# An operation list of a third annealing in a gated linear attention and mixer kernel

## The chip, the cores and the metric

The kernel runs on one core of a Trainium2 chip. The metric is the device time of one execution in microseconds; the number of a kernel is the median of its runs. Five engines work from instruction queues of their own, each strictly in order: TensorE (PE in the profile, its weight loads PEld), VectorE (DVE), ScalarE (ACT), GpSimd (POOL) and SyncE (SP), which here only issues DMAs. They meet through semaphores.

## The reference

Two parts in sequence. The first is a gated linear attention for 4 batches of 8 heads, 768 steps, 48 dimensions:

```python
f = 1.0 / (1.0 + np.exp(-f_logit))
for t in range(S):
    state = f[:, :, t, :, None] * state + np.einsum('bhd,bhe->bhde', k[:, :, t], v[:, :, t])
    y[:, :, t] = np.einsum('bhd,bhde->bhe', q[:, :, t], state)
```

The second is a mixer on the result x, laid out as 4 x 768 x 384: one two-layer product over the steps (768 to 256 and back), added to x, and one over the channels (384 to 1536 and back), added again:

```python
h = np.maximum(xt @ w_tok1, 0.0) @ w_tok2
u = x + h.transpose(0, 2, 1)
return u + np.maximum(u @ w_ch1, 0.0) @ w_ch2
```

## The kernel before

The 768 steps of a batch are cut into six chunks of 128, and two chunks make a pair P (0, 1, 2). For each batch b and pair the attention is a sequence of short operations. ScalarE forms the logarithm of the gates (lines 454 to 459). VectorE or GpSimd adds the two chunks of a pair (`two`, line 467), TensorE sums along the steps by a triangular matrix (lines 479 to 486), VectorE makes `first` (line 499), and ScalarE takes exponentials into `GG` (lines 502 and 519). VectorE multiplies q and k by them (`qk`, line 523; in the trace line 448, the helper's). The products are turned so that dimensions lie on partitions: for batches 0 and 1 by TensorE (line 546), with a copy out of PSUM into `kT` and `qT` (line 550), for batches 2 and 3 by a DMA transpose that SyncE issues (line 531). TensorE forms scores (line 581), which a mask reduces to `AmT` (lines 619 to 624: either VectorE alone, or a ScalarE copy and a GpSimd product), and the sums of k times v of each chunk (line 599). The running state goes from chunk to chunk through VectorE (line 633 for batch 0, 636 to 641 else), and is copied in two pieces into `state_bd` (line 644). The output of a pair is the product with the values (line 665) plus the terms of the state (line 657); it is copied to `x_bf` and `x_nat` (line 692).

The mixer of a batch follows: `tok1` (line 709), its ReLU into `h1T` (line 716), `tok2` (line 725), the sum u in `u_bf` (lines 736 to 751), the turn of u into `uT` in two halves of three chunks (by TensorE, line 766, for batches 0 and 1; by SyncE's DMA transpose, line 755, for batches 2 and 3), `ch1` (line 784, 24 groups of three matmuls) with its ReLU into `zT` (line 789), `ch2` (line 803, three groups of four matmuls for each chunk), the last addition on VectorE (line 814) and the store (line 818). Helper functions issue many of these, so the trace gives copies as lines 434 to 438, ReLUs as 443 and 445, two-input operations as 448 and the addition of the token mixing as 741.

All of this is written down as 1026 operations in a plan: each with the engines that may run it, what it needs, what it makes and which PSUM bank it uses. `ORDER` then says in which order they are taken and where. An entry divided by four is the number of the operation, and the remainder picks one of its possible engines:

```python
for code in ORDER:
    op = self.ops[code // 4]
    e = op.engine = op.engines[code % 4]
```

`Plan.best` goes through the list, gives every operation a start by its own costs, takes a free PSUM bank for it, and puts filler matmuls on a constant (`steady`, line 852) into early gaps of TensorE. What the chip sees of it is one queue for each engine, in the order of the list. The list is written out in the kernel; it came from an annealing that moved entries about against the same costs. Loads of GpSimd and SyncE are operations like the others, and keep among themselves the order in which the plan lists them.

Of the kernel before, what the change touches and what calls it, by code (L numbers as in the profile page):

```python
# [20 lines left out]
TURNED = 2  # L21
NQ = 2
ORDER = (
# [55 lines left out]
)  # L79
KEPT = 3  # L80
SOFT = (0, 1)
# [804 lines left out]
```

## Time and profile before

| | us |
|---|---|
| median of 3 runs | 166.11 (165.8 to 166.11) |
| profiled execution, its own time | 167.62 |
| its span, first to last instruction | 165.9 |
| TensorE busy | 158.6 |
| VectorE busy | 128.8 |
| ScalarE busy | 106.9 |
| GpSimd busy | 61.7 |

The granted TensorE clock was 0.997 of full speed over the span. Read it by stages: batch 0's attention and the loads fill the first 35 us; from then on channel products of one batch are interleaved with the attention of the next. An engine's busy time is a sum over stages with different limits, so the stages, not the sums, say what an engine's time is worth. In the lists of instructions a time is the start, the next number the length, and what stands in brackets is the idle time before it and what ended it.

### The profile page before, as it was taken

What the parts mean: (1) busy time and instruction counts of PE and PEld (TensorE: products, weight loads), DVE (VectorE), ACT (ScalarE), POOL (GpSimd) and SP (SyncE); (2) the same over time, 40 slices, a digit from 0 to 9 for tenths busy, and PEclk for the clock granted to TensorE, in tenths of its full rate; (3) what the DMA queues carried; (4) which work ended last, traced back from release to release, by engine and by line L of the source; (5) the groups of instructions that cost most, each with busy time, mean ns of one, the idle gap of its engine ahead of it and who ended that gap; (6) DMA issues with size and microseconds to landing.
All of it is one profiled execution on the core that took longest, in us unless ns stands there. A gap on an engine that the chain in (4) does not pass through costs nothing.

```text
span 165.9 us, 4990 instructions
## 1 busy us (share of the span) xinstructions
PE 158.6 (96%) x2052; PEld 101.4 (61%) x2052; DVE 128.8 (78%) x284; ACT 106.9 (64%) x231; POOL 61.7 (37%) x86
## 2 busy tenths in 40 slices
PE   7889997999999999999999999999999999999992
PEld 3356765566667766666666765665666665656661
DVE  6748997589999999998999999988599526704331
ACT  3869784797899999999948966384811511623300
POOL 7961799964776820001914514200322020000000
PEclk9999999999999999999999999999999999999998
DMA  4999999999999999457699990991900030690506
GB/s 123 219 177 171 201 210 232 168 206 227 219 225 222 225 242 142 81 98 115 133 224 128 119 155 0 106 213 50 209 19 4 0 59 16 175 325 17 177 31 206
DMA packets 68183, 24.34 MB, mean 147 GB/s; under 512 B 60896, under 2 KB 67296, under 8 KB 68160
## 3 DMA queue, kind: packets, MB, share of 16 engines
q0 software_dynamic: 41856, 13.77, 68.2%
q1 hardware_dynamic: 25776, 10.06, 28.9%
q8 instruction: 16, 0.26, 0.7%
q10 hardware_dynamic: 528, 0.20, 0.4%
q14 instruction: 7, 0.06, 0.1%
HBM read 25.17 MB, written 4.72 MB: 180 GB/s over the span
## 4 chain that ended last, share of the span: by engine, by line
PE 82%; DMA 5%; ACT 4%; DVE 4%; issue 1%; POOL 1%; DVEq 0%; ACTq 0%; POOLq 0%
PE ps L803 28%; PE ps L784 28%; DMA qk_sb<-in_q_dram 5%; PE ps L709 5%; PE ps L725 4%; PE ps L665 3%; PE ps L581 3%; PE ps L657 2%; PE ps L546 2%; PE ps L599 2%; PE ps L766 1%; PE ps L481 1%; ACT state_bd L434 1%; ACT x_nat L434 1%; DVE qk L448 1%
## 5 line engine op out<-in xcount | busy, mean ns | idle before, releaser
L803 PE MATMUL ps<-w_ch,zT 128*128 128x384 bf16 (+2 forms) x300 | 54.0, 320 | 0.0
L784 PE MATMUL ps<-uT,w_ch 128*128 128x384 bf16 x288 | 51.6, 326 | 0.0
L784 PEld LDWEIGHTS <-w_ch 128*128 128x128 bf16 x288 | 27.8, 98 | 17.6
L803 PEld LDWEIGHTS <-zT 128*128 128x128 bf16 x300 | 27.9, 98 | 17.1
L443 ACT ACTIVATE zT<-ps 128x384 bf16<-128x384 f32 x57 | 25.1, 493 | 16.3 <-PE ps L784 16.1
L624 DVE TENSOR_TENSOR AmT<-ps,mask 128x512 bf16<-128x512 f32 x44 | 28.6, 685 | 1.5 <-PE ps L581 1.2
L445 DVE TENSOR_SCALAR zT<-ps 128x384 bf16<-128x384 f32 x39 | 20.6, 553 | 10.0 <-PE ps L784 8.9
L814 DVE TENSOR_TENSOR x_nat<-x_nat,ps 128x384 f32<-128x384 f32 (+2 forms) x25 | 13.1, 534 | 10.5 <-PE ps L803 10.5
L438 POOL CAST state_bd<-state 48x192 bf16<-48x192 f32 x15 | 5.7, 377 | 28.6 <-DVE state L641 25.8
L448 DVE TENSOR_TENSOR qk<-qk_sb,GG 128x768 bf16<-128x768 bf16 x24 | 12.9, 563 | 1.3 <-DMA qk_sb<-in_q_dram 1.3
L502 ACT ACTIVATE GG<-ps 128x384 bf16<-128x384 f32 x24 | 11.2, 485 | 3.5 <-DVE first L499 2.8
L357 POOL DMA_DIRECT2D v_sb<-in_v_dram x12 | 10.7, 894 | 6.3 <-DMA w_ch<-in_moe_w_ch_dram 3.7
L434 ACT ACTIVATE x_bf<-ps 128x384 bf16<-128x384 f32 x15 | 6.9, 483 | 8.5 <-PE ps L657 8.2
L519 ACT ACTIVATE GG<-first 128x384 bf16<-128x384 f32 x24 | 11.7, 517 | 0.2
L741 DVE TENSOR_TENSOR x_nat<-x_nat,ps 128x384 f32<-128x384 f32 x21 | 10.6, 549 | 1.4 <-PE ps L725 1.2
L357 POOL DMA_DIRECT2D qk_sb<-in_k_dram x12 | 10.9, 905 | 1.6 <-POOLq L870 0.8
L434 ACT ACTIVATE u_bf<-x_nat 128x384 bf16<-128x384 f32 x12 | 5.8, 518 | 8.6 <-DVE x_nat L741 8.6
L357 POOL DMA_DIRECT2D qk_sb<-in_q_dram x12 | 10.8, 898 | 0.5 <-DMA qk_sb<-in_q_dram 0.3
L852 PE MATMUL ps<-steady 128*128 128x512 f32 (+1 forms) x20 | 9.8, 610 | 1.0 <-DVE steady L372 1.0
L438 POOL COPY qT<-qJ 128x1024 bf16<-128x1024 bf16 x3 | 3.4, 1149 | 18.8 <-ACT zT L443 18.7
L709 PE MATMUL ps<-x_bf,w_tok 128*128 128x384 bf16 x48 | 10.4, 327 | 0.0
L434 ACT ACTIVATE x_nat<-ps 128x384 f32<-128x384 f32 x20 | 9.3, 492 | 0.1
(87 smaller groups left out, 231.3 us busy)
## 6 DMA issues: line engine op xcount, KB each, us to landing
out_dram<-x_nat SPq DMA_DIRECT2D x23, 192.0 KB, 2.3
f_sb<-in_f_logit_dram POOLq DMA_DIRECT2D x9, 384.0 KB, 8.9
qk_sb<-in_k_dram POOLq DMA_DIRECT2D x12, 192.0 KB, 8.8
qk_sb<-in_q_dram POOLq DMA_DIRECT2D x12, 192.0 KB, 9.0
v_sb<-in_v_dram POOLq DMA_DIRECT2D x12, 192.0 KB, 8.9
w_ch<-in_moe_w_ch_dram POOLq DMA_DIRECT2D x2, 576.0 KB, 9.0
w_ch<-in_moe_w_ch_dram POOLq DMA_DIRECT2D x1, 1152.0 KB, 10.6
f_sb<-in_f_logit_dram SPq DMA_DIRECT2D x2, 384.0 KB, 5.8
```

Source lines behind the costliest of these rows:

```text
L357: lambda eng=eng, into=held(dst[i], P), of=runs(src, b, P): eng.dma_start(out=into, in_=of),
L434: nc.scalar.activation(out_, in_, AF.Copy, bias=0.0, scale=1.0)
L443: nc.scalar.activation(out_, in_, AF.Relu, bias=0.0, scale=1.0)
L445: nc.vector.tensor_scalar(out_, in_, 0.0, None, ALU.max)
L448: (nc.vector if op.engine == DVE else nc.gpsimd).tensor_tensor(out_, a, b_, what)
L502: add(ACT, r, lambda n=n: nc.scalar.activation(GG[i][:, 1, n], sview(), AF.Exp, bias=0.0, scale=2.0 * n - 1.0), need=["tables"] if b == 0 ...
L519: add(ACT, r, lambda n=n: nc.scalar.activation(GG[i][:, 0, n], first[i], AF.Exp, bias=0.0, scale=2.0 * n - 1.0), need=[("first", i)] + ([" ...
L624: add(DVE, r, lambda into=into, made=made, m4=m4: nc.vector.tensor_tensor(into, made(), m4, ALU.mult), need=masks, make=[("AmT", i, js, pa ...
L709: add(PE, rank("tok1", rt), lambda rt=rt, kt=kt, pm=pm: nc.tensor.matmul(banks[pm.at][:, 0:DM], lhsT=w_tok1[:, kt, rt * 128:(rt + 1) * 128 ...
L784: nc.tensor.matmul(banks[pm.at][:, 0:384], lhsT=w[:, kt, c0:c0 + 128], rhs=uT[:, th, :, kt, :], start=(kt == 0), stop=(kt == 2))
L803: nc.tensor.matmul(banks[pm.at][:, 0:n1 - n0], lhsT=zT[:, kt, tt * 128:(tt + 1) * 128], rhs=w_ch2[:, kt, n0:n1], start=(kt == 0), stop=(kt ...
L814: add(DVE, rank("ch2", tt), lambda un=un, pm=pm, n=n1 - n0: nc.vector.tensor_tensor(un, un, banks[pm.at][:, 0:n], ALU.add), make=[("x_nat" ...
```

## The change

Only the list is other: the same 1026 operations in the order of a third annealing with other random numbers and the same objective, in which SyncE's first two loads were then exchanged. On TensorE the same operations stand in another order. 44 operations move from VectorE to ScalarE and 38 from ScalarE to VectorE; 8 move from ScalarE to GpSimd and 7 back, and 2 from VectorE to GpSimd (the sums `two` of pairs 1 and 2 of batch 0). SyncE's list begins in both with the first half of batch 0's gates of pair 0, then those of pair 1 and of pair 2. Its later entries differ: in the new list the store of batch 0's chunk 3 stands earlier, that of its chunk 5 later, and the transposes of batch 3's pair 0 stand behind three stores.

In the opening VectorE's list, from the first product of q and k on, was

```
qk(P0), qk(P0), mask, state c0, kT(P0), mask, state_bd c0, qk(P1), qk(P1), two(P2), ...
```

and is now

```
qk(P0), mask, mask, qk(P0), first(P1), mask, mask, kT(P0), state c0, qT(P0), qk(P1), qk(P1), ...
```

The list itself, cut to its first and last lines:

```diff
 ORDER = (
-    0, 4, 12, 16, 24, 28, 32, 8, 20, 188, 192, 196, 36, 40, 44, 76, 68, 48, 52, 60, 208, 356, 212, 220, 64, 224,
-    236, 240, 228, 360, 364, 368, 248, 244, 216, 376, 232, 372, 380, 388, 260, 80, 84, 265, 384, 200, 88, 296,
-    252, 92, 96, 56, 300, 256, 72, 309, 304, 396, 392, 204, 312, 268, 272, 504, 408, 400, 276, 288, 404, 316,
-    292, 280, 413, 508, 512, 320, 324, 100, 104, 108, 416, 420, 516, 448, 428, 452, 536, 532, 524, 520, 461,
-    457, 544, 540, 112, 116, 120, 284, 124, 128, 132, 432, 136, 328, 332, 340, 440, 344, 464, 336, 468, 348,
...
-    4060, 4000, 4020, 4040, 4072, 4076, 4080, 4084, 4088, 4092, 4096, 4100,
+    0, 4, 12, 16, 8, 20, 24, 28, 32, 188, 192, 196, 80, 88, 92, 96, 357, 100, 104, 36, 40, 44, 48, 76, 52, 208,
+    212, 220, 216, 240, 236, 228, 224, 232, 248, 56, 64, 244, 360, 364, 368, 252, 60, 72, 256, 296, 260, 300,
+    264, 376, 388, 384, 84, 372, 304, 200, 308, 396, 392, 68, 312, 268, 272, 316, 276, 292, 288, 325, 321, 204,
+    380, 400, 408, 280, 413, 405, 108, 112, 116, 120, 124, 128, 132, 505, 284, 508, 512, 328, 332, 516, 341,
+    524, 520, 532, 536, 448, 416, 420, 336, 452, 428, 456, 528, 440, 460, 424, 540, 544, 436, 349, 136, 140,
...
+    3980, 2180, 4056, 4076, 4040, 4060, 4080, 3992, 4084, 4088, 4092, 3996, 4096, 4000, 4100,
 )
```

98 rows, old and new, of the table ORDER are left out of this document.

## The prediction

> **What bounds the kernel now.** I read the stretches first: where the matrix engine is idle decides which part of a reordering can pay at all.
>
> ```profile
> PE 158.6 (96%) x2052; PEld 101.4 (61%) x2052; DVE 128.8 (78%) x284; ACT 106.9 (64%) x231; POOL 61.7 (37%) x86
> 0.00:35.00 35.00, 30.89 (x439) 19.50 (x440) 25.74 (x71) 24.53 (x48) 27.10 (x37) 1.00 1.43 188
> 35.00:145.00 110.00, 110.00 (x1496) 70.87 (x1495) 97.20 (x202) 78.35 (x175) 34.59 (x50) 1.00 0.94 132
> 145.00:165.90 20.90, 17.67 (x121) 11.02 (x119) 5.89 (x12) 4.00 (x10) 0.00 (x0) 0.97 0.44 153
> L852 PE MATMUL ps<-steady 128*128 128x512 f32 (+1 forms) x20 | 9.8, 610 | 1.0 <-DVE steady L372 1.0
> ```
>
> The first row is the page's busy time, the next three are stretches (length; then PE, PEld, DVE, ACT, POOL busy), the last is the filler matmuls that compute nothing. From 35 to 145 us TensorE is busy 110.00 of 110.00 us at clock 1.00: nothing there can be won by order, only lost. Lost time lies ahead of 35 us (35.00 - 30.89 = 4.1 idle, 9.8 of filler) and behind the last matmul. So the second view is the chain of waits through the opening.
>
> ```profile
> 2.34 8.39 DMA qk_sb<-in_q_dram
> 10.85 1.04 DVE qk L448 x2
> 13.28 0.69 DVE kT L436
> 26.53 0.99 issue
> 28.14 0.51 PE ps L665 x32
> 28.93 0.92 PE ps L709 x5
> 29.86 0.50 ACT h1T L443
> 33.62 0.49 PE ps L766 x6
> 34.12 2.93 PE ps L784 x18
> ```
>
> Columns: start, length, what. The opening is a latency chain: batch 0's q lands at 10.73, then products, turns, the chunk-to-chunk state, the value matmuls of pair 2 (28.14), token mixing, the turns of u, and the first channel matmul at 34.12. From there TensorE is fed to the end. The end of the kernel is therefore the time of the first channel matmul, plus the TensorE work then left, plus new stalls.
>
> **The opening, step by step.** Both lists give every engine the same operations up to the landing at 10.73 in what matters: GpSimd's first five loads and SyncE's first three loads stand in the same order in both (so the exchange named in the title is one against the annealing's own result, and costs nothing here). One operation ahead of it moves: pair 1's f32 sum, 0.56 us on VectorE, goes to GpSimd behind its fifth load and delays the loads behind it. They queue for the wire anyway; I take 0.
>
> After the landing, these rows of before are the yardstick:
>
> ```profile
> 4.55 0.20 DVE L412 COPY mask<-tri 64x64 bf16<-64x64 bf16 x1
> 8.97 0.56 DVE L499 TENSOR_TENSOR first<-ps,f_sb 128x384 f32<-128x384 f32 x1 [0.96 <-PE ps L486]
> 12.37 1.02 ACT L434 ACTIVATE qT<-ps 128x1024 bf16<-128x1024 bf16 x1 [1.39 <-PE ps L546]
> 13.70 0.83 ACT L457 ACTIVATE f_sb<-f_sb 128x768 f32<-128x768 f32 x1
> 14.71 0.32 ACT L434 ACTIVATE state_bd<-ps 48x192 bf16<-48x192 f32 x1 [0.17 <-DVE state_bd L436]
> 15.08 0.34 PE L599 MATMUL ps<-v_sb,qk 64*64 64x48 bf16 x11
> 18.43 0.64 PE L581 MATMUL ps<-qT,kT 48*64 48x128 bf16 x32
> 20.28 0.72 DVE L436 CAST state_bd<-ps 48x192 bf16<-48x192 f32 x2
> 25.69 1.14 POOL L621 TENSOR_TENSOR AmT<-AmT,mask 128x512 bf16<-128x512 bf16 x1 [0.38 <-ACT AmT L619]
> 26.06 0.67 ACT L434 ACTIVATE state_bd<-ps 48x192 bf16<-48x192 f32 x2 [0.47 <-PE ps L657]
> 28.58 0.34 PE L657 MATMUL ps<-state_bd,qT 128*128 128x96 bf16 x4
> 41.79 1.22 DVE L436 COPY qT<-ps 128x1024 bf16<-128x1024 bf16 x1
> ```
>
> Three moves lengthen the chain. First, VectorE's list puts two mask copies (0.20 each) between pair 0's two products, and pair 1's `first` (0.56) and two more masks behind them; before, `first` was done at 9.5. So the second product ends at 12.3 instead of 11.9, and ScalarE, whose next exponentials need `first`, stands until 12.85. The copy of kT still starts at 13.3, as before (13.28), but qT, copied by ScalarE from 12.37 to 13.39, is now copied by VectorE behind it: 1.22 us, done at 15.4. Chunk 0's two state copies follow three exponentials on ScalarE, and the second comes behind a gate exponential (0.83): done at 15.9, before at 14.71 + 0.32 = 15.03. The next state matmuls (15.08 before) start at 15.9: 0.8 late.
>
> Second, pair 1's kT copy goes to ScalarE, behind its qT copy: 2 x 1.02 from 17.85, so pair 1's scores start at 20.2, before at 18.43: 1.8 late. Third, chunk 2's two state copies, together on VectorE before (20.28 + 0.72 = 21.0), go to ScalarE with another copy between them: done at 23.9, 2.9 late. From there chunk 4's two copies come out at 28.4, before at 26.06 + 0.67 = 26.7: 1.7 late.
>
> That is not what reaches the end. Before, pair 2's value matmuls stood behind the 0.99 us in which TensorE waited for nothing that the profile shows: they ran at 28.14, though GpSimd's last product for them was there at 25.69 + 1.14 = 26.83. With the new list that product follows a ScalarE copy at 26.1 to 26.7 and ends at 26.7 + 1.14 = 27.85; the value matmuls start at 27.9, and the last state term at 28.9, 0.3 behind the 28.58 of before. Token mixing then ends 0.4 later (h1T at 30.25 instead of 29.86). But three groups of turns of u, the nine of the first half, move behind the first channel matmuls, so the first of those starts at 33.95 instead of 34.12, with about 0.5 us more TensorE work still to do (six turns take 0.49 with their drain). Net: 0.5 - 0.15 = +0.35 us. An error of a step here is some tenths and there are a dozen on the path: -0.8 to +1.5.
>
> **The 0.99 us.** Which wait was it?
>
> ```profile
> q8 instruction: 16, 0.26, 0.7%
> ```
>
> 16 transfers of 0.26 MB together are 16 KB each, and 4104 TensorE instructions (2 x 2052) in 16 parts are 256 each. Dense stretches of small matmuls (32 in 0.51 us at 28.14) use such a part up fastest, and the gap fell in one; that it is a wait for instructions is my reading, since no semaphore stands there. In the new list that point of TensorE's stream is still pair 1's value matmuls, which start at 26.5 and then wait for nothing until 27.9: the gap is covered. If the cover is gone it costs up to 0.99. I take 0, range 0 to 1. The Trainium skill ("Runtime: NRT & Kernel Launch", Instruction fetch mechanics) says that TensorE's instructions come in blocks of 256 and that crossing a block's end is mostly hidden; by that rule this term is 0 everywhere. The trace agrees on the size of a block, not, if my reading is right, on hidden: 0.99 us here.
>
> **The long stretch, and its one tight place.** Over 35 to 145 us VectorE and ScalarE are together busy 97.20 + 78.35 of 220 us. The new list moves 44 operations from VectorE to ScalarE and 38 back, so their totals stay within a few us, and nearly every step of attention stands within 4 us of TensorE work of its old place. I summed TensorE's durations along both lists from the first channel matmul on, and looked for consumers that stand closer behind their producers than anything in the old list did.
>
> ```profile
> L443 ACT ACTIVATE h1T<-ps 128x384 bf16<-128x384 f32 x4 | 2.0, 490 | 2.7 <-PE ps L709 2.7
> 102.16 0.52 ACT L434 ACTIVATE u_bf<-x_nat 128x384 bf16<-128x384 f32 x1 [0.59 <-DVE x_nat L741]
> 102.74 3.84 SPq L755 DMA_TRANSPOSE uT<-u_bf  x2
> DMA to landing us min/median/max: 3.2/3.2/4.5
> 107.22 0.98 PE L784 MATMUL ps<-uT,w_ch 128*128 128x384 bf16 x5
> L814 DVE TENSOR_TENSOR x_nat<-x_nat,ps 128x384 f32<-128x384 f32 (+2 forms) x25 | 13.1, 534 | 10.5 <-PE ps L803 10.5
> 162.27 0.69 DVE L814 TENSOR_TENSOR x_nat<-x_nat,ps 128x288 f32<-128x288 f32 x2 [0.43 <-PE ps L803]
> ```
>
> Two stand out, both in batch 2. The second h1T copy (0.49) has only one group of four channel matmuls for cover, part of it used by the drain: +0.1 (0 to 0.3). And SyncE's turning of u's first half: before, the three u_bf copies were done at 102.68, the transpose was issued at 102.74, landed 3.2 later at 105.94, and TensorE used it at 107.22, with 1.3 to spare. In the new list the third copy stands on ScalarE behind an exponential of batch 3 that needs sums which TensorE makes at about 102.4: the copy ends at about 104.05, the transpose lands at 107.3, and its consumer stands at 107.4. Spare is 0.1. With the median landing it costs nothing, with the slowest of the four (4.5) 1.2. I take +0.15, near the median, and keep 0 to 1.2. Queued behind this transpose on SyncE is the one of the second half, which has 4 us of other channel work to hide in; ahead of it, pair-0 transposes of batch 3, which batch 1's and batch 0's stores precede, all with their data long there. Batch 3's two halves have over 1 us to spare each.
>
> **The end.** Before, the last two VectorE adds are 288 and 96 columns wide (0.69 together). In the new list a full 384-column add (0.53) takes the place of the first, and its store is 192 KB instead of 144: +0.1 (0 to 0.3).
>
> **Sum.** 0.35 + 0.1 + 0.15 + 0.1 = +0.7 us. The profiled execution took 167.62 (span 165.9); the same would take 168.3 profiled. The runs' median is 166.11, 1.5 below the profiled one, and I carry the difference over unchanged: 166.11 + 0.7 = 166.8.
>
> **Rivals.** *The opening comes out shorter.* If VectorE's additional operations and ScalarE's longer turns cost nothing on the path, the state chain keeps its old times, pair 2's value matmuls start at 26.9 as the product of 26.83 allows, and the gap of 0.99 is covered as above: -0.99 + 0.1 at the end, 165.2. For it: before waited without a reason on its path. Against: the state copies are on ScalarE's list behind long operations, in order. *The transposes come late.* With SyncE's landing at 4.5 rather than 3.2, or the copy ahead of it half a microsecond late, TensorE stops at 107.4 for 1 to 2 us: 168.3. It decides from 0.1 us of delay. For it: 3.2 to 4.5 in four cases. *Instruction waits.* In batch 1 the new list packs small matmuls closer (pair 0's value matmuls come 7.6 us of TensorE work later, among pair 1's and 2's), so by the same sums parts of 256 are used up about 5.4 us apart, where before 6.6 was the least while loads ran; one wait like the 0.99: 167.8. By the rule of the Trainium skill above there would be no such wait, and the time would be that of the forecast. *Nothing measurable.* If the opening's 0.35 is covered by errors of the same size: 166.1.
>
> **How the numbers follow.** What this kernel's runs can tell from no change is about 0.2%, 0.33 us. The forecast (a loss of 0.35 to 1.3) gets 0.42, late transposes 0.10, instruction waits 0.08, no change 0.13, the shorter opening 0.27. Faster 0.27, same 0.13, slower 0.60. The forecast's own range is 166.5 to 167.4. For 8 in 10 the range reaches from the shorter opening (165.2) to the upper bounds together: 1.5 + 0.3 + 1.2 + 0.3 = 3.3, so 169.4; the low end is set at 165.0.
>
> **What would show it.** In the profile after: qT's first copy of 1.22 on VectorE at about 14.3; the second state matmuls at 15.9; a first channel matmul within 0.8 of 33.95; PE busy short of full in the stretch 100 to 110 if the transpose is late; a wait named issue of about 1 us if it is instructions. Wrong would be a first channel matmul earlier than 33.0 or later than 35.5, or idle TensorE of over 1 us between 35 and 160 in any other place: then a wait on PSUM or on an engine's order that I have not seen decides.

## The result and the profile after

The changed kernel took 168.47 us (median; its executions 168.0 to 170.7) beside 166.0 for the kernel before: ratio 1.0141, 95% interval 1.0114 to 1.0167, or 2.3 us more. A second series, five executions beside eleven of before, gave 168.39 and 166.07, ratio 1.0131 (1.0111 to 1.0151). The forecast was +0.7, slower. Its direction and its range held; it saw a third of the size.

The execution of the changed kernel that was profiled first was a disturbed one (170.7 us, which the ratio leaves out), and in the one of before q had landed late. So both kernels were run and profiled once more, 168.67 and 165.87 us, and the comparisons below are between these two where the first profiles are not named. First the stretches (length; then PE, PEld, DVE, ACT and POOL busy, granted clock, DMA) and the group of the first channel matmuls. After:

```profile
0.00:35.00 35.00, 31.83 (x437) 20.05 (x442) 25.93 (x71) 25.08 (x50) 29.03 (x38) 1.00 1.45 190
35.00:145.00 110.00, 108.73 (x1490) 69.95 (x1488) 92.69 (x192) 80.64 (x177) 36.81 (x52) 1.00 0.99 141
145.00:166.90 21.90, 18.64 (x127) 11.60 (x125) 7.16 (x15) 4.40 (x10) 0.00 (x0) 1.00 0.29 100
L784 PE MATMUL ps<-uT,w_ch 128*128 128x384 bf16 x288 | 50.1, 326 | 1.2 <-DVE AmT L624 0.9 <-DVE zT L445 0.3
```

Before, again:

```profile
0.00:35.00 35.00, 32.33 (x448) 20.83 (x451) 27.00 (x74) 26.32 (x53) 27.91 (x37) 1.00 1.45 192
35.00:145.00 110.00, 110.00 (x1496) 70.81 (x1495) 95.94 (x199) 77.56 (x172) 33.93 (x49) 1.00 0.96 137
L784 PE MATMUL ps<-uT,w_ch 128*128 128x384 bf16 x288 | 51.6, 326 | 0.0
```

The middle stretch, in which before was fed without a gap, now has 1.27 us without a matmul, nearly all of it (1.2) ahead of channel matmuls. The opening holds less work: 437 matmuls where before had 448. Now TensorE through the opening (start, length, what; in brackets the idle time before it and its releaser). Before, again:

```profile
13.88 0.34 PE L599 MATMUL ps<-v_sb,qk 64*64 64x48 bf16 x11
24.77 0.57 PE L665 MATMUL ps<-v_sb,AmT 64*128 64x48 bf16 x31
25.75 0.18 PE L665 MATMUL ps<-v_sb,AmT 64*128 64x48 bf16 x1 [0.42 <-issue]
26.31 0.57 PE L665 MATMUL ps<-v_sb,AmT 64*128 64x48 bf16 x32
30.59 1.77 PE L766 MATMUL ps<-ident,u_bf 128*128 128x128 bf16 x18
32.19 1.63 PE L784 MATMUL ps<-uT,w_ch 128*128 128x384 bf16 x9
```

After, with three later rows:

```profile
14.12 0.34 PE L599 MATMUL ps<-v_sb,qk 64*64 64x48 bf16 x11 [0.33 <-ACT state_bd L434]
19.58 0.22 PE L657 MATMUL ps<-state_bd,qT 128*128 128x96 bf16 x1
20.21 0.30 PE L657 MATMUL ps<-state_bd,qT 128*128 128x96 bf16 x3 [0.42 <-issue]
25.35 0.57 PE L665 MATMUL ps<-v_sb,AmT 64*128 64x48 bf16 x31
26.34 0.19 PE L665 MATMUL ps<-v_sb,AmT 64*128 64x48 bf16 x1 [0.41 <-issue]
26.95 0.57 PE L665 MATMUL ps<-v_sb,AmT 64*128 64x48 bf16 x32
31.47 0.68 PE L766 MATMUL ps<-ident,u_bf 128*128 128x128 bf16 x9
32.76 0.97 PE L784 MATMUL ps<-uT,w_ch 128*128 128x384 bf16 x5
58.36 0.65 PE L784 MATMUL ps<-uT,w_ch 128*128 128x384 bf16 x3 [0.91 <-DVE AmT L624]
76.84 0.97 PE L784 MATMUL ps<-uT,w_ch 128*128 128x384 bf16 x5 [0.28 <-DVE zT L445]
99.95 0.33 PE L657 MATMUL ps<-state_bd,qT 128*128 128x96 bf16 x4
```

The first row of each is the second state product, and the last matmul of the kernel starts at 160.715 before and at 163.433 after: 2.72 us, which divide like this.

- To the second state product: 14.12 against 13.88, +0.24. In the profiles of the five kernels with the new list whose first sums were not held up (below), this time lay between 13.46 and 14.16, so this part is within the scatter.
- From there to the first channel matmul: 18.64 us against 18.31, +0.33. In it stand two waits inside a run of like matmuls, named issue, where before has one. (The bracket counts from the modelled end; from start to start the waits are 0.63 and 0.58, and 0.60 before.)
- From the first channel matmul to the last: 130.68 against 128.52, +2.16. Nine turns of u now stand behind the first channel matmul (x9 where before had x18): 0.5 us of work. The wait at 58.36 costs 0.97 (1.13 from start to start, where such matmuls stand 0.16 apart). The one at 76.84 costs 0.45 in this execution (its cause is in the last section), the one at 99.95 (TensorE waits for GpSimd's copies of `state_bd`, which end at 99.90) 0.24.
- Behind the last matmul's start: 3.51 against 3.45, next to nothing.

### The profile page after: what moved, and what is told of

Its sections match the earlier page's. It is cut to its first block, busy times and chain, and to the rows that moved or that the text cites. A ratio compares the mean times of both kernels' runs of the same rounds, so it can differ in the third digit from the quotient of the medians.

```text
span 169.0 us, 5007 instructions
## 1 busy us (share of the span) xinstructions
PE 160.4 (95%) x2054; PEld 101.8 (60%) x2054; DVE 125.4 (74%) x276; ACT 110.1 (65%) x236; POOL 65.8 (39%) x89
## 5 line engine op out<-in xcount | busy, mean ns | idle before, releaser
L803 PE MATMUL ps<-w_ch,zT 128*128 128x384 bf16 (+2 forms) x300 | 52.1, 320 | 0.0
L784 PE MATMUL ps<-uT,w_ch 128*128 128x384 bf16 x288 | 50.1, 326 | 1.1 <-DVE AmT L624 0.9
L443 ACT ACTIVATE zT<-ps 128x384 bf16<-128x384 f32 x64 | 29.2, 494 | 16.3 <-PE ps L784 16.3
L624 DVE TENSOR_TENSOR AmT<-ps,mask 128x512 bf16<-128x512 f32 x44 | 29.1, 683 | 2.5 <-PE ps L581 2.5
L445 DVE TENSOR_SCALAR zT<-ps 128x384 bf16<-128x384 f32 x32 | 17.0, 550 | 8.3 <-PE ps L784 8.3
L448 DVE TENSOR_TENSOR qk<-qk_sb,GG 128x768 bf16<-128x768 bf16 x24 | 13.7, 588 | 3.2 <-DMA qk_sb<-in_q_dram 2.7
L438 POOL CAST state_bd<-state 48x192 bf16<-48x192 f32 x16 | 6.2, 385 | 25.5 <-DVE state L641 19.4
L438 POOL COPY qT<-qJ 128x1024 bf16<-128x1024 bf16 x5 | 6.1, 1224 | 19.0 <-DMA qJ<-qk 18.9
L852 PE MATMUL ps<-steady 128*128 128x512 f32 (+1 forms) x22 | 11.8, 650 | 1.0 <-DVE steady L372 1.0
L725 PE MATMUL ps<-h1T,w_tok 128*128 128x384 bf16 x48 | 9.4, 325 | 0.2
```

What stands on the lines that cost most here:

```text
L438: nc.gpsimd.tensor_copy(out_, in_)
L443: nc.scalar.activation(out_, in_, AF.Relu, bias=0.0, scale=1.0)
L445: nc.vector.tensor_scalar(out_, in_, 0.0, None, ALU.max)
L448: (nc.vector if op.engine == DVE else nc.gpsimd).tensor_tensor(out_, a, b_, what)
L624: add(DVE, r, lambda into=into, made=made, m4=m4: nc.vector.tensor_tensor(into, made(), m4, ALU.mult), need=masks, make=[("AmT", i, js, pa ...
L725: nc.tensor.matmul(banks[pm.at][:, 0:DM], lhsT=w_tok2[:, kt, tt * 128:(tt + 1) * 128], rhs=h1T[:, kt, :], start=(kt == 0 and not held), st ...
```

## The late glast

The wait at 58.36 is not for a result that the matmul uses. Its PSUM bank is held by scores that VectorE has not yet reduced. VectorE's rows, and SyncE's DMA issues, after:

```profile
55.45 0.55 DVE L448 TENSOR_TENSOR qk<-qk_sb,GG 128x768 bf16<-128x768 bf16 x1
57.34 0.36 DVE L641 TENSOR_TENSOR state<-tsum,glast 128x192 f32<-128x192 f32 x1 [1.34 <-DMA glast<-ends]
57.62 0.68 DVE L624 TENSOR_TENSOR AmT<-ps,mask 128x512 bf16<-128x512 f32 x1
51.02 1.82 SPq L515 DMA_DIRECT2D glast<-ends  x3
```

VectorE stands 1.34 us for the chunk decays (`glast`) of batch 1's pair 1, with the reduction queued behind. The new list has the one DMA of pair 2's `glast` ahead of pair 1's two, and that one waits for `ends` of pair 2. So the three are issued together from 51.02 on. The test moved one entry (1396 is pair 1's `glast`):

```diff
-    ... 1448, 1144, 1556, 1396, 1452, 1156 ...
+    ... 1448, 1144, 1396, 1556, 1452, 1156 ...
```

> The kernel after, unchanged, as the yardstick for the next three: about 168.3 us, first channel matmul at 34.9, two waits of TensorE without a semaphore at about 21.5 (0.8 us) and 27.6 (0.6 us), and one wait of about 1.1 us ahead of a channel matmul at about 59.5. Both theories say the same here.

> The list of after with one entry moved on SyncE alone: the two DMAs of batch 1, pair 1's glast stand ahead of pair 2's one DMA instead of behind it, so they are issued at about 51.7 instead of 53.7 and land at about 57.5 instead of 60. Theory: the 1.1 us ahead of the channel matmul at 60.5 is VectorE standing in its state update for that landing, with the product that frees the matmul's PSUM bank queued behind; the wait goes, and the time falls by 0.8 to 1.1 us. Rival: the wait belongs to the bank's product itself (VectorE is simply too busy there), then 0 to 0.3 us.

Measured: 168.39 for the unchanged list; with the entry moved 167.76, ratio to before 1.0093 (1.0057 to 1.0129). Its trace (line numbers one lower):

```profile
48.38 2.31 SPq L514 DMA_DIRECT2D glast<-ends  x3
54.80 0.35 DVE L640 TENSOR_TENSOR state<-tsum,glast 128x192 f32<-128x192 f32 x1
L783 PE MATMUL ps<-uT,w_ch 128*128 128x384 bf16 x288 | 50.1, 326 | 0.3 <-DVE zT L444 0.3
```

The DMAs leave 2.6 us earlier (1.5 of it from the moved entry, since this execution's first channel matmul starts 1.1 earlier, at 31.64), VectorE does not wait, the wait of 0.9 is gone, and from the first channel matmul to the last it takes 129.71 instead of 130.68: -0.97. The medians differ by 0.63, which is less sharp, because executions of this list scatter by 2 us (166.55 to 168.51). The theory holds; the rival, a busy VectorE, would have left the wait. The order alone does not fix the price: with SyncE's order unchanged TensorE lost 0.84 to 1.16 us there in four traces, and nothing in a fifth, that of the 66 tiny matmuls below, where VectorE stood only 0.42 us for this `glast`.

## Where a block of instructions ends

The two waits of the opening have no releaser. The theory was that TensorE's stream comes in parts of 256 instructions. Then what matters is where a part ends, and instructions that do nothing, put ahead, move that place and nothing else.

The first try took fillers away and put tiny matmuls in:

```diff
+    small = [66]
     def idle(n):
+        if small:
+            n -= 4 * 1
...
+        for _ in range(small.pop() if small else 0):
+            nc.tensor.matmul(banks[NBANK - 1][0:64, 0:48], lhsT=steady[0:64].broadcast_to((64, 64)),
+                             rhs=steady[0:64].broadcast_to((64, 48)), start=True, stop=True)
```

> The list of after; one float32 filler matmul (two instruction pairs) at the very start of TensorE's work is replaced by 66 tiny ones, so that every later instruction stands 128 instructions, half a 16 KB block, further down TensorE's stream. Theory instructions: the two waits without a semaphore at 21.5 and 27.6 sit at the ends of blocks of 256; with the ends elsewhere (about 12, 20, 26 and 33 us) each block of the opening takes more than 6 us to use up, the waits are gone or fall under 0.3 us together, the first channel matmul starts at 34.0 to 34.3 instead of 34.9 and the time falls by 0.6 to 0.9 us. Theory chain (the opening is later only because the state copies stand behind longer work on ScalarE and VectorE): first channel matmul at 34.9 within 0.15, time within 0.2 us of the kernel after.

> The same with 132 tiny matmuls in place of two float32 fillers (four pairs): every later instruction stands 256 further down, a whole block, so the ends of the blocks fall where they fell in after. Theory instructions: both waits are back at 21.5 and 27.6 within 0.3 us, first channel matmul at 34.9 within 0.2, time as the kernel after within 0.25 us, and longer than with 128. Theory chain: as the kernel after as well, and as with 128.

With 66, both waits are gone, and from the second state product to the first channel matmul it takes 17.65 us instead of 18.64: as forecast. The time is not: the tiny matmuls end at 7.5, the first sums start at 7.44 instead of 6.53, and the executions scatter from 167.85 to 176.15 (median 170.27), so no gain can be read from them. With 132 it is no control at all:

```profile
3.43 7.23 PE L858 MATMUL ps<-steady 64*64 64x48 bf16 x132
10.59 1.65 PE L479 MATMUL ps<-two,tri 128*128 128x384 f32 x2
```

132 take 7.23 us, and the f32 sum behind them takes 1.65 where the unchanged list's took 0.81: TensorE was at half its rate. Time 175.03. Nothing on blocks follows from it.

So the next kernels used no-operations, which TensorE's sequencer runs while the fillers occupy the array:

```diff
+    spare = [40, 0, 0, 24]
     def idle(n):
...
+        for _ in range(spare.pop(0) if spare else 0):
+            nc.tensor.nop(hint="keep", nofuse=True)
```

> The kernel before, unchanged, profiled again, because its first profiled execution (167.62 us) stood 1.5 above its runs: about 166.1 us, q of pair 0 landed at 8 to 8.7 us instead of 10.7, first channel matmul at 32.0 to 32.6, the wait without a semaphore of 0.99 us still there, ahead of the value matmuls of pair 2. If the late landing of q made that wait, it is gone.

> The list of after with 64 no-operations put in at the same places (40 behind the first filler, 24 behind the fourth). Theory instructions: both waits without a semaphore (0.63 and 0.58 in the unchanged list) are gone or under 0.3 together; from chunk 0's second state matmuls to the first channel matmul 17.4 to 18.0 us instead of 18.64; time 167.3 to 167.8. Theory chain: both waits stay, 18.6 us, time 168.4 within 0.3.

> The list of before with 64 no-operations put into TensorE's stream ahead of the first dense work (40 behind the first filler, 24 behind the third), where TensorE waits or runs fillers: no work is added or taken away, but the ends of the 256-instruction blocks fall 64 instructions earlier in the work. Theory instructions: ends at about 13, 18.6 and 24.6 us, each block takes about as long as its refill, the wait of 0.99 is gone or under 0.3, the time falls by 0.3 to 0.9 us. Theory chain: the wait stays, time within 0.2 us of the kernel before.

Before again: 166.11, and the wait is still there (0.60). After with 64: 167.89, ratio 1.0088 (1.0054 to 1.0122); both waits are gone and the stretch takes 17.87 us instead of 18.64. TensorE's rows at the two places:

```profile
19.75 0.34 PE L657 MATMUL ps<-state_bd,qT 128*128 128x96 bf16 x4
25.23 0.57 PE L665 MATMUL ps<-v_sb,AmT 64*128 64x48 bf16 x32
26.23 0.57 PE L665 MATMUL ps<-v_sb,AmT 64*128 64x48 bf16 x32
32.03 1.79 PE L784 MATMUL ps<-uT,w_ch 128*128 128x384 bf16 x10
```

x4 and x32 without a break, where after had x1 and x3, and x31 and x1. The median moved by 0.5, less than the 0.6 to 1.1 expected, and is blunt for the same scatter (166.42 to 169.30). Before with 64: 166.09, ratio 1.0002 (0.9985 to 1.0019), no gain, a miss. Its trace shows what came in the place of the wait:

```profile
25.60 0.57 PE L665 MATMUL ps<-v_sb,AmT 64*128 64x48 bf16 x32
59.04 0.32 PE L665 MATMUL ps<-v_sb,AmT 64*128 64x48 bf16 x11
59.74 0.43 PE L665 MATMUL ps<-v_sb,AmT 64*128 64x48 bf16 x21 [0.39 <-issue]
```

The wait of the opening is gone (18.00 us for the stretch instead of 18.31), and a new one stands in batch 1 at 59.74. The first is TensorE's record 696 in before (weight loads and matmuls counted together, no-operations not), the second is record 1656, which is 696 - 64 + 4 x 256. It is the same kind of end, four parts on. (This profiled execution took 166.77, 0.7 above its median, so what it lost need not be what the median lost.)

The control is a number of no-operations that puts an end in a worse place, 48, only 16 fewer:

> The list of after with 48 no-operations (24 behind the first filler, 24 behind the fourth), 16 fewer than the 64 that took both waits away. Theory instructions: a block's end now falls just ahead of pair 1's scores, and the block before it is used up in 4.4 us where its refill takes 5.8: one wait of 1.2 to 1.6 us at 18.5 to 20 us, without a semaphore, and none at 26; from chunk 0's second state matmuls to the first channel matmul 18.3 to 18.9 us, against 17.87 with 64; time 168.0 to 168.8. Rival (it is the no-operations themselves that smooth the stream, not where a block ends): as with 64, no wait, 17.9 us, time 167.5 to 168.0.

> The list of after with 48 no-operations once more, for its trace, since the first one's profiled execution ran TensorE at under half its rate from end to end and its time (167.6) stood against the theory of instructions, which had asked for 168.0 to 168.8. Theory instructions, with the place named: the waits of the unchanged list stand at TensorE's records 443 and 696 (loads and matmuls counted together, no-operations not); with 48 ahead they must stand at 395 (inside pair 1's scores, at about 18.9 us) and, if at all, at 648 (in the turns of pair 2 or its scores, 24 to 25.5 us); the first is 0.8 to 1.6 us long, or it is hidden because the scores are waited for late. Rival (block ends do not matter, the waits of after were something else): they stand at 443 and 696 as before, or there are none.

The first of the two took 167.6, against the theory; its profiled execution took 321 us, with TensorE slow from end to end, and can't be read. The second took 167.31, ratio 1.0075 (1.0045 to 1.0105), and its trace has one wait:

```profile
18.12 0.34 PE L581 MATMUL ps<-qT,kT 48*64 48x128 bf16 x8
19.09 0.30 PE L581 MATMUL ps<-qT,kT 48*64 48x128 bf16 x6 [0.63 <-issue]
25.18 0.57 PE L665 MATMUL ps<-v_sb,AmT 64*128 64x48 bf16 x32
```

It stands at record 396, where 395 was named ahead (443 - 48), in the middle of pair 1's scores; at 443, 648 and 696 there is none. The place is right, and both rivals are out: the wait moved along the stream by the number of no-operations, less one. The size was wrong: 0.84 from start to start instead of 1.2 to 1.6 (at the low end of the second expectation), and the times, 167.6 and 167.31, lie below the 168.0 to 168.8 asked for, and below the 167.89 with 64, which has no such wait at all. So the medians of this list do not resolve waits of this size; what is shown is their place.

Nor is their length fixed. The kernel with the moved `glast` entry has TensorE's stream of after, unchanged, and its trace has the two waits at the same records, 443 and 696, but shorter:

```profile
18.92 0.64 PE L656 MATMUL ps<-state_bd,qT 128*128 128x96 bf16 x4
24.59 0.82 PE L664 MATMUL ps<-v_sb,AmT 64*128 64x48 bf16 x32
```

0.64 and 0.82, where 64 no-operations left 0.34 and 0.57; from start to start the waits are 0.34 and 0.24 instead of 0.63 and 0.58, and the stretch takes 18.18 us instead of 18.64.

The start of each transfer on the instruction queue, as the trace has it, stands at one distance from the end of the wait that it ends:

```
kernel             record   transfer starts   wait ends   between
before again        696          23.43           25.75      2.32
after again         443          17.98           20.21      2.23
after again         696          23.91           26.34      2.43
after, 48 no-ops    396          16.62           19.09      2.47
before, 64 no-ops  1656          57.35           59.74      2.39
```

From the end of the part before to the end of the wait it is 5.4 to 6.1 us in these five (14.47 to 20.21 and 20.21 to 26.34 in after, 20.02 to 25.75 in before, 13.73 to 19.09 with 48, 53.92 to 59.74 in batch 1), most of it ahead of the transfer. A part that is used up faster than that made TensorE wait at these places. But the length of a part does not decide alone: in before with 136 no-operations (below) one was used up in 5.13 us (53.47 to 58.60, TensorE busy throughout, DMA at 219 GB/s) without a wait. Its transfer started 1.6 us behind the end of the part before, where in the five above it was 2.9 to 3.7; why it started sooner is open. The Trainium skill ("Runtime: NRT & Kernel Launch", Instruction fetch mechanics) says that the next page is fetched while the present one runs and that the cost of crossing is mostly hidden. This case agrees with the first (the transfer at 17.98 starts while TensorE still works, until 19.80) and not, in dense stretches beside loads, with the second: 0.24 to 1.17 us each from start to start in the traces, at records that can be named ahead.

Two more numbers of no-operations failed as tests, because the no-operations themselves came onto the path.

> The same with 192 no-operations (96, 24 and 72), so that a block ends inside the 64 matmuls of pair 2's values. Theory instructions: no wait at about 20 and none of the two that after shows, but a new one of 1.2 to 2.0 us in or right behind pair 2's value matmuls at 26 to 28 us, since the block ahead of it is used up in about 4 us; 18.4 to 19.2 us from the second state matmuls to the first channel matmul; time 168.0 to 169.0 if the no-operations themselves delay nothing. Theory chain: as with 64, no new wait there.

> The list of before with 136 no-operations (30 behind each of the three float32 fillers of the start, 16 behind the second filler call, 30 behind the third), so that neither the opening nor batch 1 has a block that is used up in under 5.8 us: by the counts in its trace the wait at 25.4 goes and the one that 64 no-operations brought at 59 does not come. Theory instructions: no wait over 0.2 at either place, time 165.4 to 165.8, faster than both kernels. Rivals: the wait of before was covered by the product that the value matmuls wait for, 166.0 to 166.2; or the no-operations delay the first sums by 0.3 us or more and the gain is lost, 166.0 to 166.6.

```profile
18.32 0.46 PE L599 MATMUL ps<-v_sb,qk 64*64 64x48 bf16 x10 [2.95 <-issue]
20.00:30.00 10.00, 9.53 (x114) 6.95 (x113) 6.20 (x13) 5.21 (x12) 5.86 (x6) 0.50 1.10 197
```

With 192, 72 no-operations behind the fourth filler kept TensorE idle for 2.95 us. In this profiled execution (177.18 us) the granted clock from 20 to 30 us was 0.50, so no part was used up fast there and the wait asked for could not come. The median is 173.25, and nothing is shown. With 136 in before, neither wait is there, but the first sums start at 7.84 (6.24 in before again):

```profile
7.84 1.45 PE L479 MATMUL ps<-two,tri 128*128 128x384 f32 x4
```

166.89, ratio 1.0053 (1.0031 to 1.0075): the second rival, a loss. So no version here beats before.

## Both causes together

> The list of after with both of its foreseen causes taken away: batch 1's pair-1 glast ahead of pair 2's on SyncE, and 72 no-operations in TensorE's stream (16 behind each of the three float32 fillers of the start, 24 behind the fourth filler call). Theory (the 2.3 us are 0.5 of work moved behind the first channel matmul, 0.6 to 0.7 of instruction waits, 1.0 of the late glast and 0.2 to 0.5 of small waits): 168.4 - 1.0 - 0.65 = 166.75, between 166.4 and 167.1, still 0.3 to 1.0 slower than the kernel before. Rival (the list is slower throughout, and a wait taken away comes back elsewhere): 167.3 or more.

166.87, ratio 1.0044 (1.0019 to 1.0070): 1.5 us of the 2.3 gone, where 1.65 was forecast, and slower than before, as forecast. What is left, 0.8 us, holds the 0.5 of moved work and the wait for `state_bd` (0.25 in its trace). Its profiled execution (167.60) has neither instruction wait nor late glast, but lost time in a third way (last section).

## Why the prediction was right or wrong

**What bounds the kernel** was read rightly: the end is the first channel matmul, plus the work then left, plus new stalls, and the 2.72 us divide so without a rest worth naming.

**The opening, step by step.** The early steps came as written: in the first profile after, where the first product of q and k began 0.19 later than in before (11.04), qT's copy on VectorE took 1.21 and ended at 15.63 (15.4 predicted), the second state product stood at 16.07 (15.9), pair 1's scores at 20.45 (20.2), chunk 2's copies ended at 23.77 (23.9). From the second state product to the first channel matmul the prediction had 18.05 us (33.95 - 15.9). It is 17.87 where 64 no-operations take both instruction waits out, and 18.64 in after again, so this part holds but for the waits. The net of it, -0.15 to the first channel matmul, did not come: that matmul starts 0.57 later in after again (32.76 against 32.19), and at 34.90 in the first profile, 0.95 behind the predicted 33.95. The yardstick was wrong too: 34.12 is where a piece of the chain starts, and in the same trace the row of the first channel matmuls starts at 33.96. The 0.5 us of work moved behind was right.

**The 0.99 us** is the first step that failed. The reading, a wait for instructions, was right. "The gap is covered" was not: the term went in at 0. The cover was to be pair 2's last product on GpSimd, which the prediction had end 1.35 behind the start of pair 1's value matmuls (27.85 - 26.5). In after again:

```profile
25.19 1.15 POOL L621 TENSOR_TENSOR AmT<-AmT,mask 128x512 bf16<-128x512 bf16 x1 [2.10 <-ACT AmT L619]
```

It ended at 26.34, 0.99 behind that start (25.35), and pair 2's value matmuls stood at 26.95, 0.6 later: TensorE was late, not the product. The new list has two such waits in place of one, and they cost it 18.64 - 17.87 = 0.77, against 18.31 - 18.00 = 0.31 in before: +0.46, inside the range given for the term (0 to 1). Each of these lengths is from one execution, and the same streams took 18.18 and 18.83 (new list) and 18.88 (before) in others, so 0.46 is an estimate. That a late crossing of one end makes the next refill late, so that the wait moves along with the work meant to hide it, is an argument that no run tried.

**The long stretch** is the second, and larger, failure: +0.25 was given to two places in batch 2, neither of which waits in after again, and the stretch cost 1.66 beside the moved work. The step "looked for consumers that stand closer behind their producers" followed results; it did not follow SyncE's queue in batch 1, where a DMA for pair 1 stood behind one for pair 2, nor who holds the PSUM bank of a channel matmul. 0.97 of it is that one exchange, shown by the kernel that undoes it. The prediction's own test (over 1 us idle between 35 and 160 in another place: a wait on PSUM or on an engine's order not seen) pointed there. The 0.45 at 76.84 (0 to 0.5 in the other profiles of this list) is read from traces in the last section; the 0.24 at 99.95 was not tried. The tight place that the prediction did name was read rightly. In after again the transpose was issued at 104.83, so with the 3.2 us of before's median it lands at 108.03, and TensorE used it at 108.21. In the kernel with 66 tiny matmuls it was late:

```profile
107.40 0.82 PE L784 MATMUL ps<-uT,w_ch 128*128 128x384 bf16 x4 [0.32 <-DMA uT<-u_bf]
```

**The end**: +0.1 was given, next to nothing came.

**The rivals.** Instruction waits were priced as one of 0.99 in batch 1, where a part was to be used up in about 5.4 us. It took 5.97 (50.05 to 56.02), and batch 1 had no such wait in this list; they came in the opening, and 64 no-operations gave one in batch 1 to the other list. Late transposes came only in that one trace, with 0.5 us from start to start instead of 1 to 2. A shorter opening and no change did not come.

**The sum.** It was low because two terms stood at nothing: the wait called covered (0.46 in these traces), and any stall in the long stretch outside batch 2 (1.66). The upper bounds that were added up, 3.3, held neither of them; the result lay in the range because the opening was allowed to be 1.5 late and batch 2's transpose 1.2. So the range held in part by luck, and the direction rests on 0.5 foreseen of 2.3.

## What to carry to other kernels

Where a matrix engine runs hundreds of small matmuls beside heavy loads, count its instructions: here it waited at ends of parts of 256 that it used up faster than the 5.4 to 6.1 us measured to the end of the wait, though not at every such end (5.13 us above), and at places that any edit ahead of them moves. Compare two orders only after looking for waits without a releaser in both. And when reading a new order, follow each DMA queue as an engine of its own: a small DMA behind one whose data come later holds up a vector engine, and through a PSUM bank the matrix engine, microseconds on.

## What else the runs showed of the hardware

An operation of VectorE can be held for the length of one on GpSimd. In the kernel with both causes removed:

```profile
14.48 1.00 POOL L447 TENSOR_TENSOR two<-f_sb 128x384 f32<-128x384 f32 x1
14.53 1.03 DVE L407 COPY mask<-tri 64x128 bf16<-64x128 bf16 x1
80.98 1.15 POOL L437 COPY qT<-qJ 128x1024 bf16<-128x1024 bf16 x1 [1.61 <-DMA qJ<-qk]
81.05 1.50 DVE L469 TENSOR_TENSOR two_lo<-two 128x384 bf16<-128x384 f32 x1
```

The mask copy took 1.03 (0.23 in after again) and `two_lo` 1.50 (0.56), each begun 0.05 to 0.07 behind a GpSimd operation and ended 0.08 and 0.42 behind its end. The Trainium skill ("SBUF — State Buffer", SBUF: two separate sides) has it that these two engines share a pair of ports, and that a GpSimd operation, or one of VectorE in a two-port mode or with two inputs in SBUF, holds the pair for its whole instruction if it starts first. The two pairs of rows agree; in which mode the mask copy runs no row shows. The first pair made the opening of that execution long, 18.59 us although it had no instruction wait: TensorE waited 0.6 us from start to start for the scores that the mask reduces, until 17.94.

The same explains the wait at 76.84. In after again, and then with 48 no-operations (the second time), where that wait does not stand:

```profile
74.28 1.15 POOL L438 COPY qT<-qJ 128x1024 bf16<-128x1024 bf16 x1 [15.44 <-DMA qJ<-qk]
74.39 1.93 DVE L448 TENSOR_TENSOR qk<-qk_sb,GG 128x768 bf16<-128x768 bf16 x2
73.69 1.01 DVE L448 TENSOR_TENSOR qk<-qk_sb,GG 128x768 bf16<-128x768 bf16 x2
```

Two products take 1.01 us there, and 1.93 where GpSimd's copy began 0.11 ahead of the first; the ReLU (`zT`) for which TensorE then waits stands right behind them on VectorE. Over the traces of this list the two go together: products of 1.01, 1.76, 1.93 and 1.98 us, waits of 0, 0.27, 0.45 and 0.50. Before's products took 1.02. The order of the two starts depends on a few tenths of a us; that it makes part of this list's scatter is an argument only, and no run moved one of these operations.

A no-operation costs TensorE's sequencer at least 2.95 / 72 = 0.041 us.
